# First q and k loads with long runs, one transfer a tile, and the heads turned by a product each

## The chip, the cores and the metric

The kernel runs on one core of one Trainium2 chip. The metric is device microseconds of one launch. Three runs of the kernel before gave 815.03, 815.05 and 818.45 us, median 815.05.

## The reference, cut to what matters

Windowed attention (batch 4, 8 heads, 576 positions, head size 64) feeds two MLPs of 2304 tokens, one after the other. The first four heads of a batch see the last 32 positions, the other four every fourth of the last 128.

```python
scores = scale * np.matmul(q, k.transpose(0, 1, 3, 2))
scores = np.where(masks[None, :, :, :], scores, -1000000000.0)
attn = softmax(scores)                      # written out in the reference
attn_out = np.matmul(attn, v)
x = attn_out.transpose(0, 2, 1, 3).reshape(B * S, H * D)
h = x @ w_in; g = np.maximum(0.01 * h, h); x = g @ w_out
a = x @ w1; b = x @ w2; out = ((a * b) @ w3) @ w_out2
```

q, k and v come as 32-bit floats, the weights as 64-bit floats, which the kernel turns into pairs of 32-bit parts (high and low).

## The kernel before

Two heads make a pair and share the 128 partitions, 64 for each. A batch has four pairs: two of the dilated kind, two plain ones. For the first batch the kernel loads q and k by `load_qk`: eight tiles (q and k of four pairs, m = 0 to 7), each of 288 KB, by two DMAs, one for each head (L345). On n partitions (72 for the dilated pairs, 96 for the plain ones) lie c rows of each head (8 or 6), the two heads side by side in every row, so that each run of the transfer is one head's row of 64 floats, 256 bytes. `turn_rows` then turns such a tile so that the head size lies on the partitions: one TensorE transposition for each c (L397), 128 wide, both heads at once, 8 or 6 a tile, into a pair of PSUM banks; a copy on ScalarE or VectorE (L404) takes it to `qT` or `kT`. Later batches use other functions (`load_halves`, `turn_halves`).

Each pair is worked in two rounds (rows 0 to 319 and 320 to 575), so the first batch has eight rounds n = 0 to 7: scores by products (L420, `ps_s`), mask and scale on VectorE (L435), the maximum (L440), the exponential on ScalarE (L448 in one piece after a subtraction on GpSimd, or L456 in pieces), the sum, its reciprocal, the division on GpSimd (L469), a transposition on TensorE (L485, `ps_p`), a copy (L489), and the products with v (L506, `ps_o`). The result goes into `x` as a high part (L529) and a low part (L532).

Beside this the weights' blocks are loaded (`load_cols` L141 for w_in, `load_rows` L138 for w_out) and converted: a scaling (L113, or L111 on ScalarE), two steps on ScalarE (L165, L167), a shift (L154), an addition (L171), and then the two parts (L116, L118). As soon as four x tiles and the first blocks are there, the products of the first MLP begin (L126 to L128, first into `ps_early`).

The order on every engine is written out by hand: the string `START` has one letter for each step, and each engine takes its steps in that order. `L` takes the next load of the string `LOADS`; `~` is a product of the identity with itself whose result nobody reads (L1503, `warm`); `T` and `Y` are the two halves of `turn_rows`; `S M X q E w` the steps of the scores, `V x y` those of the values, `Q` an early product of the MLP. Loads go out on SyncE's queue (SP), but for the tile that `ON_SCALAR` names, q of the third pair, whose two DMAs ScalarE issues. Strings like `X_ON`, `P_ON` and `MLP_CONV` say which engine makes a step (A ScalarE, D VectorE, G GpSimd).

In what follows T0 to T7 are the eight turns of the first batch, in the order q, k of the first pair, q, k of the second, and so on, and S0 to S7 and V0 to V7 the scores and values of the eight rounds; on TensorE they come as T0 T1 S0 T2 S1 T3 S2 T4 S3 T5 V0 V1 T6 S4 T7 S5 V2 S6 S7 V3 ... V7.

Of the kernel before, what the change touches and what calls it, by code (L numbers as in the profile page):

```python
# [8 lines left out]
F32 = mybir.dt.float32  # L9
# [19 lines left out]
def tile_window_attention_two_mlps(  # L29
# [14 lines left out]
    nc = tc.nc  # L44
    P = 128
    B, H, S, D = q.shape
# [5 lines left out]
    NF = F1 // P  # L52
# [77 lines left out]
    def parts(t, *idx):  # L130
        return tuple(t[(slice(None), i, *idx)] for i in range(2))

    def rows(t, off, dims):
        return bass.AP(t.tensor, t.offset + off, dims)


    def load_rows(raw, src, i):
        nc.sync.dma_start(raw, src[i * P : (i + 1) * P, :])  # L138

    def load_cols(raw, src, i):  # L140
        nc.sync.dma_start(  # L141
            raw.rearrange("p (c f) -> p c f", f=P),
            src[:, i * P : (i + 1) * P].rearrange("(c p) f -> p c f", p=P),
        )
# [29 lines left out]
    def run(steps):  # L174
# [3 lines left out]
    engine_of = {"A": nc.scalar, "D": nc.vector, "G": nc.gpsimd}  # L178
    FOLD_CONV = ("GAD",)
    P_ON = "AADAAAAADAADDDAAAAAAAAAAAAAAAAAA"  # L180
    X_ON = "AADADADDADADDAAAAAAAAAAAAAAAAAAA"
    ONE_EXP = (0, 1, 3, 6, 11, 13, 16, 17, 19, 20, 27, 28, 29, 31)
    GS_ON = {
# [7 lines left out]
    }  # L191
    TURN_ON = "AAAADDAA"
    MLP_CONV = (
        "GDG DAG DDD DAD DAD DAD AAD DDD DAD AAD DAG DAD DAG DAD DAD GAD "
        "AAD AAD AAD DDD GAG AAG GAG DDD AAD ADD GAD DAD DAD AAD AAD GAD "
        "GAD GAD GAD GAD GAD GAD GAD GAD"
    ).split()
    LAST_CONV = ("AAD",)
# [1107 lines left out]
    with ExitStack():  # L1306
# [54 lines left out]
        for f in range(NF + AHEAD):  # L1361
# [14 lines left out]
        runs += [(c, 0, NF) for c in range(2, NCH)]  # L1376
        turns = [(c, f, f0, f1) for c, f0, f1 in runs for f in range(f0, f1)]
        START = (
            "~~~L~L~~~~LTLL~Y~~TY~~~SLTMXSY~LqTMXLE~q~Y~wESRNPwTRML~XNCSYLqEwPMTCLXLVVYqxRxTyEwNy"
            "SYLTRLMLNXLY~LqEPCSPGDwMVALRXCSNLxBL~MqyEwPUSVGLXCLRq~AM~DxVNEy~BXwPqEwGL~R~D~N~Cx~G"  # L1380
            "RADPNyVCIVBUPOx~LCy~IVxUGQQQHOyAxyDIBQQQHAGLOBUAHLUIOgclgIcDJBOgGlLUAHDIFHGAcglBOcHB"
            "LUlgLIDHGLgOAUGHDgIAGHOBDALUBGJDILUBOILJUcLAOlBGGJgclLAIHBDOZgAczUHBlDIGgUJAOIDGBOJc"
            "DAJcBlUGlHIcDlAOgJBDUgLGUJLIcUAlIHOBDLOIUJgGOIJAGBOHALDcclGBDUlAJDIUBOHgIcLGZUzlHAOI"
            "DBGJgUAOgcJIDlcBGOALHBlUGFJgcLABDLlSILUSLOMHXDqEwIMHFgcXHGLlLgDAOqEwJRGUNAJIRDBNcOBP"
            "UJgLGcIAUOBHDIGCAHgOBlcDlGPUgHAlIDUBJOILUGOJCcGAgDlIBDOAHcLUBlIJUgOILO|JcFHlLSSMVMVg"
            "clJXxqEywXFHqxLREyNHgwcRlPgNJCFLPZHczlCHggFVVxLJxLyyJclFJLclSLSMXHMqEwXJqgRcHENwlPgR"
            "HcNClPgJCVclVxyJxGyADBULJHIOgclHGHgDAclBHgULIOJgHZczlSgGSMADHXMBXqEwLUHIOgRqEwNHGRPJ"
            "ANCDBPcULJClIOgJclVVcgGxHAlyxDBGyULHADIOgBHULIOJLJclgGJcADlBJcglLUHcIOlHgHgGJADBJULc"
            "FIOJlLcglHcLlJgHclFSSMMJgLclHXFHgqXLHgqEwHERwNJRNFJcLlJcglJgcFlLHZczlHJgPgFCLHclHgSS"
            "MJFXLJcqEwMlXPFHCqgLRJEcNwlJcRglNVcVxlJyxyPclHCSgSMXHMqXPgEHCwqEwRNHVgRNVxLHyxyPJCLS"  # L1390
            "clSMgFJXLMJqEwcFPlXLJCcRlqEwNJcglRJcNlVFxVxHyLyLPgJCclPFHCLVgcxVlyJxyLHHgclHSgSgMHXM"
            "qEwXRHqEwNPRJCNScSlMFMJgLHZczFPJClXLXqEwVclRgxVLxNyygqEwRNFJPcJClFHgJclSclSMHMXXqPgq"
            "HECwERwNVgxVRyJxLyNPcHlCPgHCSSMVMVHXqEwXqRExNxJywyRNPcJlCPcJClVV^LLLLLLLpgrgclprprJ0"
            "01Jd1dc2Ll23LxHyxy3HJgc4gl0561d2Wc3LlW4prLpH0561L2d45grWW6L0L3d12W3Jp44LrWp0Jr51L6d2"
            "Wclpr0pL5r6dL1L2WeLfH33pr4pWg0L5drLHL6142c3LlgHWpWrpWr540L61d2L03pgrpL5HrW61JL2dJLpc"
            "rLlgWclWp3rWLp4erL5H0f61d2W3LJ4gprLLpHri5c0jl61k2dWg3LmWJp4pLr05r61L2cdWl3LWp4prW0L5"
            "rH61L2d3LWpWpgLHr4r50eL6fd142W0p3561rdWpr24JH3cLWlW56pLrpLgrL4W56pWrprWW!JeLLfLJcLlJ"
            "caglboJchlLnHaHobhgclJnL7g8J9$cla%bHo&h*nLH+-agcblJ=o<hngJLca7l8boH9$h%JnL&gclaH*ob+"
            "hJ-n=gc<Hla7boHhgcl8L9$JnL%a&gbJco*lh+HLnHg-=J<c7al8ob9hH$nLgH%a&gocl*b+Jg-Hh=cnL<li"
            "aH7j8kgH9boh$nLm%aJ&boc*h+JlncL-lJg=g<Hc7al8ob9H$h%gnLJ&a*obJ+-chJl=Lng<cHalc7blHo8h"  # L1400
            "9$nJ%a&bJ*oh+gJn-cg=Hlc<l7H8g9$cH%gl&J*+-Jc=l<@JstgHclvssJgctlHvtvJgsscltJvJ#tsvtivj"
            "km"
        )
        LOADS = (
            "0123a45b67wcwwwwdww8wwwwwwwwwwwwwwwwwew9AwwwwwwwBfCDEFwghwwwwwwwiGHIjJKLMNOPklQRoSTp"
# [53 lines left out]
        with tc.manual_schedule():  # L1459
# [5 lines left out]
            for x in START:  # L1465
                if x == "L":
                    y = next(feed)
                    if y == "w":
                        conv.fetch()
                    elif y == "y":  # L1470
                        conv3.fetch()
                    elif y == "z":
                        load_wo2(next(wo2_no))
                    elif y == "x":
                        conv4.fetch()
                    elif y in "rs":
                        load_y("rs".index(y))
                    elif y in QK:
                        load_qk(QK.index(y))
                    else:  # L1480
                        load_v("abcdefghijklmnop".index(y))
                elif x == "|":
                    raw_es.close()
                    gs_es, gs_p = pool("gs", "left")
                    gs_t.append(gs_p.tile([P, 6 * HM], F32R, name="gs"))
                elif x == "^":
                    att_es.close()
                    fold_es, fold = pool("fold", "right")
# [73 lines left out]
```

## Time and profile before

| | us |
|---|---|
| median of three runs | 815.05 |
| the profiled execution's own time | 814.0 |
| its span | 812.2 |
| TensorE busy | 798.0 (98%) |
| VectorE busy | 535.8 (66%) |
| ScalarE busy | 418.2 (51%) |
| GpSimd busy | 195.9 (24%) |
| first product of the MLP starts | 40.06 |

In the span's 40 slices of 20.3 us TensorE is busy for 8 tenths in the first two and for 9 or more from then on, but for the last (7). The chain that ended last is 82% TensorE. The page's list of queues has nearly all bytes on one of them (173.69 of 175.79 MB), which takes 69.5% of the sixteen DMA engines' time. Busy time on TensorE includes the products that nobody reads.

### The profile page before, as it was taken

How to read it: one execution, taken by the hardware profiler on the slowest of the kernel's cores; microseconds unless marked ns; L12 is line 12 of the kernel's file. 1: busy time of each engine (PE TensorE's matmuls, PEld its weight loads, DVE VectorE, ACT ScalarE, POOL GpSimd, SP SyncE). 2: the span in 40 equal slices, each digit the busy share in tenths (PEclk: the TensorE clock that was granted, in tenths of full speed). 3: DMA queues.
4: the chain of work that ended last, by engine and by line, in shares of the span. 5: the costliest groups of instructions: out<-in, count | busy, mean ns of one | idle time of the engine just before them, and what ended most of it. 6: DMA issues, size and time to landing. Idle time of an engine off the chain costs nothing.

```text
span 812.2 us, 16134 instructions
## 1 busy us (share of the span) xinstructions
PE 798.0 (98%) x5806; PEld 774.1 (95%) x5806; DVE 535.8 (66%) x1063; ACT 418.2 (51%) x954; POOL 195.9 (24%) x223
## 2 busy tenths in 40 slices
PE   8899999999999999999999999999999999999997
PEld 7799999999999999988989999999999999999997
DVE  4899997553555354567784777567869658466446
ACT  4799983452134352556664677554555235333341
POOL 4404421343332334431312210000110300121013
PEclk9999999999999999999999999999999999999999
DMA  6996846346552531477856789539999999889884
GB/s 154 254 322 210 258 116 187 94 143 174 136 155 68 136 102 27 131 175 216 241 174 232 258 277 302 200 112 338 358 382 375 304 305 308 253 253 284 301 253 89
DMA packets 162831, 175.79 MB, mean 216 GB/s; under 512 B 67520, under 2 KB 116160, under 8 KB 162752
## 3 DMA queue, kind: packets, MB, share of 16 engines
q1 hardware_dynamic: 158368, 173.69, 69.5%
q10 hardware_dynamic: 4384, 1.08, 0.6%
q8 instruction: 46, 0.75, 0.4%
q14 instruction: 33, 0.27, 0.1%
HBM read 137.89 MB, written 36.83 MB: 215 GB/s over the span
## 4 chain that ended last, share of the span: by engine, by line
PE 82%; ACT 5%; DVE 4%; SPq 3%; DMA 3%; issue 2%; POOL 0%; ACTq 0%; DVEq 0%; POOLq 0%
PE ps_x L126 7%; PE ps_h L126 7%; PE ps_x L127 7%; PE ps_x L128 7%; PE ps_h L127 7%; PE ps_h L128 7%; PE ps_b L127 3%; PE ps_b L126 3%; PE ps_b L128 3%; PE ps_s L420 2%; PE ps_o L506 2%; PE ps_a L126 2%; PE ps_a L127 2%; PE ps_a L128 2%; PE ps_p L485 2%
## 5 line engine op out<-in xcount | busy, mean ns | idle before, releaser
L126 PE MATMUL ps_h<-x,win 128*128 128x384 f32 (+2 forms) x440 | 139.5, 317 | 0.0
L128 PE MATMUL ps_h<-x,win 128*128 128x384 f32 (+2 forms) x440 | 137.5, 313 | 0.0
L127 PE MATMUL ps_h<-x,win 128*128 128x384 f32 (+2 forms) x440 | 137.5, 312 | 0.0
L126 PE MATMUL ps_x<-gs,wout 128*128 128x384 f32 (+2 forms) x356 | 114.5, 322 | 0.0
L128 PE MATMUL ps_x<-gs,wout 128*128 128x384 f32 (+2 forms) x356 | 112.4, 316 | 0.0
L127 PE MATMUL ps_x<-gs,wout 128*128 128x384 f32 (+2 forms) x356 | 112.4, 316 | 0.0
L118 POOL TENSOR_TENSOR gs<-g,gs 128x384 fp32r<-128x384 f32 (+2 forms) x69 | 65.8, 953 | 146.5 <-DVE gs L116 138.1
L577 ACT ACTIVATE g<-ps_h 128x384 f32<-128x384 f32 (+2 forms) x110 | 48.1, 438 | 100.6 <-PE ps_h L128 72.3
L126 PEld LDWEIGHTS ps_h<-x,win 128*128 128x128 f32 x440 | 83.1, 189 | 1.3
L127 PEld LDWEIGHTS ps_h<-x,win 128*128 128x128 f32 x440 | 83.1, 189 | 0.3
L128 PEld LDWEIGHTS ps_h<-x,win 128*128 128x128 f32 x440 | 83.1, 189 | 0.0
L118 POOL TENSOR_TENSOR p<-t,p 128x384 fp32r<-128x384 f32 x12 | 12.6, 1046 | 256.8 <-DMA place<-ws_dram 96.5
L126 PEld LDWEIGHTS ps_x<-gs,wout 128*128 128x128 f32 x356 | 67.1, 189 | 1.2
L127 PEld LDWEIGHTS ps_x<-gs,wout 128*128 128x128 f32 x356 | 67.2, 189 | 0.3
L128 PEld LDWEIGHTS ps_x<-gs,wout 128*128 128x128 f32 x356 | 67.1, 189 | 0.0
L116 DVE CAST gs<-g 128x384 fp32r<-128x384 f32 (+2 forms) x70 | 24.6, 352 | 57.7 <-PE ps_x L128 43.0
L456 ACT ACTIVATE s<-s,nmax 128x96 f32<-128x96 f32 x83 | 30.0, 364 | 21.8 <-DVE nmax L440 21.7
L127 PE MATMUL ps_b<-ys,place 128*128 128x384 f32 x120 | 40.2, 335 | 0.7 <-DVE ys L118 0.7
L126 PE MATMUL ps_b<-ys,place 128*128 128x384 f32 x120 | 40.1, 334 | 0.0
L128 PE MATMUL ps_b<-ys,place 128*128 128x384 f32 x120 | 40.1, 334 | 0.0
L435 DVE SCALAR_TENSOR_TENSOR s<-ps_s,masks 128x384 f32<-128x384 f32 (+2 forms) x40 | 19.8, 512 | 28.3 <-PE ps_s L420 27.9
L469 POOL TENSOR_TENSOR s<-s,rec 128x480 f32<-128x480 f32 (+1 forms) x32 | 30.0, 939 | 31.1 <-DVE rec L467 27.1
(253 smaller groups left out, 2115.9 us busy)
## 6 DMA issues: line engine op xcount, KB each, us to landing
place<-ws_dram SPq DMA_DIRECT2D x140, 256.0 KB
place<-wps_dram SPq DMA_DIRECT2D x84, 256.0 KB
ws_dram<-ws SPq DMA_DIRECT2D x24, 512.0 KB
raw<-in_moe_w_in_dram SPq DMA_DIRECT2D x16, 512.0 KB
raw<-in_moe_w_out_dram SPq DMA_DIRECT2D x16, 512.0 KB
rawf<-in_moe_w_dram SPq DMA_DIRECT2D x64, 128.0 KB
wo2f<-wo_dram SPq DMA_DIRECT2D x32, 256.0 KB
rawl<-in_moe_w_dram SPq DMA_DIRECT2D x16, 512.0 KB
```

The lines of the kernel that those rows point to most:

```text
L116: copy_on(e_hi)(hi, src)
L118: e_lo.tensor_tensor(lo, src, hi.bitcast(F32), op=ALU.subtract)
L126: nc.tensor.matmul(ps, a[1], b[0], start=first, stop=False, skip_group_check=seeded)
L127: nc.tensor.matmul(ps, a[0], b[1], start=False, stop=False, skip_group_check=seeded)
L128: nc.tensor.matmul(ps, a[0], b[0], start=False, stop=last, skip_group_check=seeded)
L420: nc.tensor.matmul(ps[j * QB : (j + 1) * QB, i - bl.start], qt[d, i * QB : (i + 1) * QB], kt[d, first_key(i, plain) : first_key(i, plain) ...
L435: nc.vector.scalar_tensor_tensor(s[:, a:z], ps[:, a:z], SCALE, mk, op0=ALU.mult, op1=ALU.add)
L456: nc.scalar.activation(s[:, i], s[:, i], AF.Exp, bias=nmax[:, i : i + 1], accum_out=total[:, i : i + 1])
L469: nc.gpsimd.tensor_tensor(s, s, rec[:, :nb].unsqueeze(2).to_broadcast([P, nb, KB]), op=ALU.mult)
L485: nc.tensor.transpose(pss[g][:, i - i0], s[:, i], ident)
L506: nc.tensor.matmul(ps[j * D : (j + 1) * D, i * QB : (i + 1) * QB], vt[i][:, h + j, :], t[:, i, j * QB : (j + 1) * QB], start=True, stop=True,)
L577: nc.scalar.activation(g, ps, AF.Prelu, alpha=SLOPE)
```

## The change

`load_qk` keeps the two heads apart in the tile (`[P, 2, 8, D]` in place of `[P, 8, 2, D]`) and brings both by one DMA, whose runs are a partition's c rows of one head in one piece: 2 KB for the dilated pairs, 1.5 KB for the plain ones. Since a head's row no longer lies beside the other's, `turn_rows` has a product with the identity for each head and row, 64 wide, into its own 64 partitions: 16 or 12 products in place of 8 or 6 transpositions. ScalarE issues three of the eight tiles now (q of the first pair, q and k of the last); the others go out on SP. Four of the 31 products that nobody reads are left out, some letters of `START` stand elsewhere, two casts of x (rounds 4 and 7) go from VectorE to ScalarE (`X_ON`), and four blocks of weights share their conversion among the engines in another way (`MLP_CONV`).

```diff
+    ON_SCALAR = ("k3", "q0", "q3",)
...
     def load_rows(raw, src, i):
-        nc.sync.dma_start(raw, src[i * P : (i + 1) * P, :])
+        block_queue[0].dma_start(raw, src[i * P : (i + 1) * P, :])
...
-    X_ON = "AADADADDADADDAAAAAAAAAAAAAAAAAAA"
+    X_ON = "AADAAADAADADDAAAAAAAAAAAAAAAAAAA"
...
-        "GDG DAG DDD DAD DAD DAD AAD DDD DAD AAD DAG DAD DAG DAD DAD GAD "
-        "AAD AAD AAD DDD GAG AAG GAG DDD AAD ADD GAD DAD DAD AAD AAD GAD "
+        "GDG DAG DDD DAD DAD DDG AAD DDD DAD AAD DAG DAD DAD DAD DAD DAD "
+        "AAD ADD AAD DDD GAG AAG GAG DDD AAD ADD GAD DAD DAD AAD AAD GAD "
...
-    ON_SCALAR = ("q2",)
...
-        t = win_p.tile([P, 8, 2, D], F32, tag="win", name=f"{nm}{pi}", bufs=NF)
-        for j in range(2):
-            queue_of(nm + str(m // 2)).dma_start(
-                t[:n, :c, j, :], rows(src, o + j * S * D, [[c * D, n], [D, c], [1, D]])
-            )
+        t = win_p.tile([P, 2, 8, D], F32, tag="win", name=f"{nm}{pi}", bufs=NF)
+        queue_of(nm + str(m // 2)).dma_start(
+            t[:n].rearrange("p j c d -> p j (c d)")[:, :, : c * D],
+            rows(src, o, [[c * D, n], [S * D, 2], [1, c * D]]),
+        )
...
-                src = t[:n, g * (c // 2) + c1].rearrange("p j d -> p (j d)")
-                nc.tensor.transpose(ps[:, g, c1 * n : (c1 + 1) * n], src, ident[:n, :n])
+                for j in range(2):
+                    nc.tensor.matmul(
+                        ps[j * D : (j + 1) * D, g, c1 * n : (c1 + 1) * n],
+                        t[:n, j, g * (c // 2) + c1], ident[:n, :n], start=True, stop=True,
+                    )
...
         START = (
-            "~~~L~L~~~~LTLL~Y~~TY~~~SLTMXSY~LqTMXLE~q~Y~wESRNPwTRML~XNCSYLqEwPMTCLXLVVYqxRxTyEwNy"
+            "~~~L~L~~~~LTLL~Y~TY~SLTMXSMYLqTX~LEq~Y~wESRNPwTRMSL~XNYCLqEwPMTCLXLVVYqxRxTyEwNyLSYL"
...
                     if y == "w":
+                        block_queue[0] = queue_of(f"w{conv.fetched}")
                         conv.fetch()
+                        block_queue[0] = nc.sync
```

`queue_of("w0")` and so on name no tile of `ON_SCALAR`, so the weights' blocks stay on SP.

TensorE at its start, before: the turns are L397 (`ps_qT`, `ps_kT`), the scores L420 (`ps_s`).

```order
L1503 MATMUL warm<-ident 128x128 x8
L397 MATMUL ps_qT_182<-ident,q_168 128x72 x8
L1503 MATMUL warm<-ident 128x128 x3
L397 MATMUL ps_kT_208<-ident,k_172 128x72 x8
L1503 MATMUL warm<-ident 128x128 x3
L420 MATMUL ps_s_222<-kT_217,qT_204 64x96 x10
L397 MATMUL ps_qT_236<-ident,q_179 128x72 x8
L420 MATMUL ps_s_249<-kT_217,qT_204 64x96 x8
L1503 MATMUL warm<-ident 128x128
L397 MATMUL ps_kT_265<-ident,k_191 128x72 x8
```

The same place now (the lines are 2 to 6 higher):

```order
L1509 MATMUL warm<-ident 128x128 x8
L399 MATMUL ps_qT_179<-ident,q_168 64x72 x16
L1509 MATMUL warm<-ident 128x128 x2
L399 MATMUL ps_kT_211<-ident,k_171 64x72 x16
L1509 MATMUL warm<-ident 128x128
L425 MATMUL ps_s_231<-kT_228,qT_208 64x96 x10
L399 MATMUL ps_qT_244<-ident,q_177 64x72 x16
L425 MATMUL ps_s_265<-kT_228,qT_208 64x96 x8
L399 MATMUL ps_kT_281<-ident,k_196 64x72 x16
```

A turn has 16 instructions where it had 8 and four products that nobody reads are gone.

ScalarE at its start, before: the copies L404 of the first turns and, between the second and the third, the two loads L345.

```order
L404 ACT_TABLE_LOAD
L404 COPY qT_204<-ps_qT_182 128x576
L404 COPY kT_217<-ps_kT_208 128x576
L345 DMA q_233<-in_q_dram 96x6x64 x2
L404 COPY qT_258<-ps_qT_236 128x576
L448 ACTIVATE s_245<-s_245 128x480
```

ScalarE at its start now:

```order
L346 DMA q_168<-in_q_dram 72x2x512
L409 ACT_TABLE_LOAD
L409 COPY qT_208<-ps_qT_179 128x576
L409 COPY kT_228<-ps_kT_211 128x576
L409 COPY qT_276<-ps_qT_244 128x576
L453 ACTIVATE s_261<-s_261 128x480
L409 COPY kT_310<-ps_kT_281 128x576
L453 ACTIVATE s_274<-s_274 128x384
L346 DMA q_367<-in_q_dram 96x2x384
```

The load between the copies is gone; one stands ahead of everything else, and two later ones behind the exponentials of the first two rounds.

SP from its start to the first block of weights (L141), before:

```order
L345 DMA q_168<-in_q_dram 72x8x64 x2
L345 DMA k_172<-in_k_dram 72x8x64 x2
L345 DMA q_179<-in_q_dram 72x8x64 x2
L345 DMA k_191<-in_k_dram 72x8x64 x2
L381 DMA v_0_194<-in_v_dram 96x4x64 x2
...
L345 DMA k_261<-in_k_dram 96x6x64 x2
...
L345 DMA q_330<-in_q_dram 96x6x64 x2
L345 DMA k_351<-in_k_dram 96x6x64 x2
L141 DMA raw_378<-in_moe_w_in_dram 128x4x128
```

SP now, to the same block (L149):

```order
L346 DMA k_171<-in_k_dram 72x2x512
L346 DMA q_177<-in_q_dram 72x2x512
L346 DMA k_196<-in_k_dram 72x2x512
L383 DMA v_0_198<-in_v_dram 96x4x64 x2
...
L346 DMA q_242<-in_q_dram 96x2x384
L346 DMA k_278<-in_k_dram 96x2x384
...
L149 DMA raw_410<-in_moe_w_in_dram 128x4x128
```

Fourteen issues of q and k stood ahead of the first block of weights; five do now. The v loads between them are the same twelve.

## Rows read from the trace of the kernel before

**Rows 1.** The page's busy time of each engine.

```profile
PE 798.0 (98%) x5806; PEld 774.1 (95%) x5806; DVE 535.8 (66%) x1063; ACT 418.2 (51%) x954; POOL 195.9 (24%) x223
```

**Rows 2.** Windows: stretch, length, busy PE, PEld, DVE, ACT, POOL; clock, DMA share, GB/s.

```profile
30.00:40.00 10.00, 8.87 (x129) 7.14 (x123) 9.37 (x27) 8.16 (x27) 5.28 (x5) 1.00 1.08 260
40.06:812.19 772.13, 764.68 (x5368) 745.82 (x5364) 508.84 (x992) 393.69 (x878) 177.39 (x185) 1.00 0.70 217
```

**Rows 3.** Timeline of TensorE: start, us, line, op, shape [idle before, releaser].

```profile
5.48 0.69 PE L397 MATMUL ps_qT<-ident,q 72*128 72x72 f32 x8 [0.61 <-DMA q<-in_q_dram]
6.01 0.88 PE L1503 MATMUL warm<-ident 128*128 128x128 f32 x6
...
8.69 1.04 PE L420 MATMUL ps_s<-kT,qT 64*64 64x96 f32 x20
9.67 0.72 PE L397 MATMUL ps_qT<-ident,q 72*128 72x72 f32 x8
...
12.32 0.73 PE L397 MATMUL ps_kT<-ident,k 72*128 72x72 f32 x8 [0.70 <-ACT qT L404]
...
13.77 1.04 PE L420 MATMUL ps_s<-kT,qT 64*64 64x96 f32 x20
...
15.89 0.66 PE L397 MATMUL ps_qT<-ident,q 96*128 96x96 f32 x6
16.38 0.41 PE L1503 MATMUL warm<-ident 128*128 128x128 f32 x2
...
18.60 1.27 PE L506 MATMUL ps_o<-pT,v 96*64 96x64 f32 x36
20.57 0.69 PE L397 MATMUL ps_qT<-ident,q 96*128 96x96 f32 x6 [0.70 <-DVE x L532]
...
23.66 1.04 PE L420 MATMUL ps_s<-kT,qT 64*64 64x96 f32 x20
...
25.20 0.80 PE L506 MATMUL ps_o<-pT,v 96*64 96x64 f32 x20
27.32 0.88 PE L420 MATMUL ps_s<-kT,qT 64*64 64x96 f32 x16 [1.32 <-DVE total L464]
...
31.64 0.80 PE L506 MATMUL ps_o<-pT,v 96*64 96x64 f32 x20
32.38 0.49 PE L1503 MATMUL warm<-ident 128*128 128x128 f32 x2
...
37.58 0.78 PE L506 MATMUL ps_o<-pT,v 96*64 96x64 f32 x8 [0.39 <-DMA v<-in_v_dram]
...
40.06 0.41 PE L126 MATMUL ps_early<-x,win 128*128 128x320 f32 x1
```

**Rows 4.** Timeline of SP's queue: start, us, line, load, count.

```profile
0.74 1.92 SPq L345 DMA_DIRECT2D q<-in_q_dram  x2
...
16.68 1.24 SPq L345 DMA_DIRECT2D q<-in_q_dram  x2
17.97 1.30 SPq L345 DMA_DIRECT2D k<-in_k_dram  x2
19.32 0.62 SPq L141 DMA_DIRECT2D raw<-in_moe_w_in_dram  x1
```

**Rows 5.** Timeline of ScalarE, with the loads that it issues (ACTq).

```profile
6.21 0.64 ACT L404 COPY qT<-ps_qT 128x576 f32<-128x576 f32 x1 [4.19 <-PE ps_qT L397]
...
9.57 2.02 ACTq L345 DMA_DIRECT2D q<-in_q_dram  x2
11.63 0.64 ACT L404 COPY qT<-ps_qT 128x576 f32<-128x576 f32 x1 [2.99 <-PE ps_s L420]
```

**Rows 6.** Timeline of GpSimd near 26 us.

```profile
25.42 0.67 POOL L113 TENSOR_SCALAR pair<-raw 128x512 f32<-128x512 f32 x1 [2.31 <-DMA raw<-in_moe_w_in_dram]
```

**Rows 7.** Timeline of VectorE, at 26 and at 34 us.

```profile
26.12 0.43 DVE L154 TENSOR_SCALAR pair<-pair 128x512 int32<-128x512 int32 x1 [1.64 <-POOL pair L113]
...
34.26 0.48 DVE L529 CAST x<-ps_o 128x320 fp32r<-128x320 f32 x1
```

More of the change, by code (lines that the diff above doesn't have):

```diff
@@ L131, in parts, with queue_of @@
         return tuple(t[(slice(None), i, *idx)] for i in range(2))
+    ON_SCALAR = ("k3", "q0", "q3",)
+    def queue_of(name):
+        return nc.scalar if name in ON_SCALAR else nc.sync
+    block_queue = [nc.sync]
     def rows(t, off, dims):
@@ L137, in load_rows @@
     def load_rows(raw, src, i):
-        nc.sync.dma_start(raw, src[i * P : (i + 1) * P, :])
+        block_queue[0].dma_start(raw, src[i * P : (i + 1) * P, :])
     def load_cols(raw, src, i):
-        nc.sync.dma_start(
+        block_queue[0].dma_start(
             raw.rearrange("p (c f) -> p c f", f=P),
@@ L270, in tile_window_attention_two_mlps @@
     nat_t, v_t, qk_t = {}, {}, {}
-    ON_SCALAR = ("q2",)
-    def queue_of(name):
-        return nc.scalar if name in ON_SCALAR else nc.sync
     order, seq = [], []
@@ L1378, in tile_window_attention_two_mlps @@
         START = (
-            "~~~L~L~~~~LTLL~Y~~TY~~~SLTMXSY~LqTMXLE~q~Y~wESRNPwTRML~XNCSYLqEwPMTCLXLVVYqxRxTyEwNy"
[L1380 to L1402, printed above, removed]
+            "~~~L~L~~~~LTLL~Y~TY~SLTMXSMYLqTX~LEq~Y~wESRNPwTRMSL~XNYCLqEwPMTCLXLVVYqxRxTyEwNyLSYL"
+            "TRLMLNXYLqEPCSPGwLDMVARXCNSLxBL~~MqyEwPUSVGLXCLRq~AM~DxVNE~BXwPqEwGGL~Ry~D~N~Cx~RADP"
@@ new lines, in tile_window_attention_two_mlps @@
+            "NyVCIVBUPOx~LCy~VxUGQQQIHOyAxyIDBQQQHALOBUGUAHLIOgclgIcDJBOgGAlLUHDIFHGAcglBOcHBLUlg"
+            "LIDHGLgOAUGHDgIAGHOBDALUBGJDILUBOILJUcLAOlBLGJgclGIAHDBOZgAczHlUIDGBgJUAODIGBJOcADJc"
+            "BlUGlHIcDlAOgJBDUgLGUJLIcUAlIHOBDLOIgUGOIAGBOHALJJDcclGBDUlAJDIBOHgcULIGZUzlHAOIDBGJ"
+            "JgUAOgcIDlcBGOAHLBlUGFgcLABDLJlSILUSLOMHXDqEwIMHFgcXHGLlLgDAOqEwJRGUNAJIRDBNcOBPUJgL"
+            "GcIAUOBHDIGCAHgOBlcDlGPUgHAlIDUBJOILUGOJCcGAgDlIBDOAHcLUBlIJUgOILO|JcFHlLSSMVMVgclJX"
@@ new lines, in tile_window_attention_two_mlps @@
+            "xqEywXFHqxLREyNHgwcRlPgNJCFLPZHczlCHggFVVxLJxLyyJclFJLclSLSMXHMqEwXJqgRcHENwlPgRHcNC"
+            "lPgJCVclVxyJxGyADBULJHIOgclHGHgDAclBHgULIOJgHZczlSgGSMADHXMBXqEwLUHIOgRqEwNHGRPJANCD"
+            "BPcULJClIOgJclVVcgGxHAlyxDBGyULHADIOgBHULIOJLJclgGJcADlBJcglLUHcIOlHgHgGJADBJULcFIOJ"
+            "lLcglHcLlJgHclFSSMMJgLclHXFHgqXLHgqEwHERwNJRNFJcLlJcglJgcFlLHZczlHJgPgFCLHclHgSSMJFX"
+            "LJcqEwMlXPFHCqgLRJEcNwlJcRglNVcVxlJyxyPclHCSgSMXHMqXPgEHCwqEwRNHVgRNVxLHyxyPJCLSclSM"
@@ new lines, in tile_window_attention_two_mlps @@
+            "gFJXLMJqEwcFPlXLJCcRlqEwNJcglRJcNlVFxVxHyLyLPgJCclPFHCLVgcxVlyJxyLHHgclHSgSgMHXMqEwX"
+            "RHqEwNPRJCNScSlMFMJgLHZczFPJClXLXqEwVclRgxVLxNyygqEwRNFJPcJClFHgJclSclSMHMXXqPgqHECw"
+            "ERwNVgxVRyJxLyNPcHlCPgHCSSMVMVHXqEwXqRExNxJywyRNPcJlCPcJClVV^LLLLLLLpgrgclprprJ001Jd"
+            "1dc2Ll23LxHyxy3HJgc4gl0561d2Wc3LlW4prLpH0561L2d45grWW6L0L3d12W3Jp44LrWp0Jr51L6d2Wclp"
+            "r0pL5r6dL1L2WeLfH33pr4pWg0L5drLHL6142c3LlgHWpWrpWr540L61d2L03pgrpL5HrW61JL2dJLpcrLlg"
@@ new lines, in tile_window_attention_two_mlps @@
+            "WclWp3rWLp4erL5H0f61d2W3LJ4gprLLpHri5c0jl61k2dWg3LmWJp4pLr05r61L2cdWl3LWp4prW0L5rH61"
+            "L2d3LWpWpgLHr4r50eL6fd142W0p3561rdWpr24JH3cLWlW56pLrpLgrL4W56pWrprWW!JeLLfLJcLlJcagl"
+            "boJchlLnHaHobhgclJnL7g8J9$cla%bHo&h*nLH+-agcblJ=o<hngJLca7l8boH9$h%JnL&gclaH*ob+hJ-n"
+            "=gc<Hla7boHhgcl8L9$JnL%a&gbJco*lh+HLnHg-=J<c7al8ob9hH$nLgH%a&gocl*b+Jg-Hh=cnL<liaH7j"
+            "8kgH9boh$nLm%aJ&boc*h+JlncL-lJg=g<Hc7al8ob9H$h%gnLJ&a*obJ+-chJl=Lng<cHalc7blHo8h9$nJ"
@@ L1403, in tile_window_attention_two_mlps @@
+            "%a&bJ*oh+gJn-cg=Hlc<l7H8g9$cH%gl&J*+-Jc=l<@JstgHclvssJgctlHvtvJgsscltJvJ#tsvtivjkm"
         )
```

## The prediction

> **What bounds the kernel now.** I read the page's busy times first: TensorE works for 798.0 of 812.2 us, and no other engine for more than two thirds [rows 1]. The windows then say where the rest is: from 40.06 us, where the first product of the MLP starts, to the end TensorE is busy for 764.68 of 772.13 us, at a granted clock of 1.00 [rows 2]. None of the edits takes work from that stretch (the letters that move there and the four conversion patterns shift work among engines that TensorE doesn't wait for). So the change can move the end only by moving the start of the MLP, and its worth is read from the first 40 us alone.
>
> In these 40 us the timeline of TensorE is a row of short pieces with idle time between them, and three kinds of stop show: for q or k to land (0.61 us at 5.48), for ScalarE (0.70 at 12.32), and 1.32 us at 27.32 [rows 3]. The queues say why. SP issues one load after the other from 0.74 us on, and the first block of weights is the 27th, at 19.32 [rows 4]; ScalarE stands in its own two loads from 9.57 to 11.59 while a turned tile waits for its copy, which starts at 11.63 [rows 5]; and the block issued at 19.32 reaches GpSimd at 25.42 after 2.31 us of idling [rows 6], so VectorE gets its word at 26.12 after 1.64 us [rows 7], and the scores at 27.32 come late by it. The change goes at all three. What it pays with is TensorE's time.
>
> **Price of a turn.** Eight transpositions take 0.53 us from their start to the next instruction (5.48 to 6.01), six of the 96-wide ones 0.49 (15.89 to 16.38) [rows 3]. The new products do not occur in the trace. The nearest are the values: a product from 96 partitions into one 64-wide half, the halves in turn, as the new ones; ten of 64 columns take 0.74 us (31.64 to 32.38), 74 ns each. The scores have 64 partitions and 96 columns: ten in 0.98 us (8.69 to 9.67), 98 ns [rows 3]. Between the two, 72 columns are about 80 ns and 96 are 98, so a turn is 16 x 80 = 1.28 us or 12 x 98 = 1.18, dearer by 0.75 or 0.69: 4 x 0.75 + 4 x 0.69 = 5.76 us more on TensorE. Against it stand four dropped products that nobody reads, at most 0.29 us each (three in 0.88 [rows 3]), which filled waiting time in any case. Ends for the price: from below a turn costs what it costs now (the halves run wholly beside each other); from above, a product has the price of a full-width one, (0.88 - 0.16) / 3 = 0.24 us for 128 columns, where 0.16 is what a group's last instruction adds (0.69 - 0.53). By width that is 0.135 or 0.18 us, 2.16 us a turn. I take 1.28 and 1.18, since the values' rows have the same halves.
>
> The Trainium skill, "FP8 and Floating Point Precision", section "TensorE Precision Notes", has a rule that speaks against the change: true 32-bit products take four passes through the array. As an estimate by that page a turn of 16 products would be 16 x 4 x 72 columns at 2.4 GHz = 1.92 us; the sum below would come out some 5 us later, as in the costly rival. The trace does not agree for products in halves: at four passes one of 64 columns would be 107 ns, and the row has 74.
>
> **The chain, stage by stage.** *To the first scores.* T0 could start at 4.87 (5.48 less 0.61 of waiting) if q landed by then. Both tiles' loads now go out side by side, from ScalarE and from SP, with one issue each where q alone took two, 1.92 us [rows 4], so I take that it does; at worst it starts at 5.48 as now. Then T0 1.28 + 0.16, copy 0.64 with 0.04 ahead of it (5.48 + 0.69 = 6.17, copy at 6.21 [rows 5]) to 6.99; T1, which waits for that copy, 7.03 to 8.47; copy to 9.15; S0 at 9.2. Now it is 8.69: **0.5 later**. The longer turns stand one behind the other here and eat what the loads give.
>
> *To S2.* T2 starts 0.98 after S0, at 10.2, and ends at 11.6; ScalarE is free, so its copy starts at 11.66, where it starts at 11.63 today. T3 at 12.34 (today 12.32), done at 13.8, copied at 14.46, S2 at 14.5 (today 13.77): **0.7 later**. The removed stop on ScalarE has paid for T2 and no more.
>
> *To S5.* Two 96-wide turns lie ahead of the first values: + 1.38, less up to 1.0 of idle and of a dropped filler there, so V0 comes 1.1 to 2.1 after today's 18.60. T6 stops today for 0.70 us; the view names VectorE, but its tile's loads were issued until 17.92, and 17.92 + 2.8 (5.48 - 2.66, the same lag as at the first tile) = 20.7, which is its start [rows 3, 4]. That stop goes. T6 and T7 add 1.38, one filler goes (0.25). S5: 23.66 + 1.5 to 2.6.
>
> *To S6.* Here the raw block is paid back. Of the 14 issues of q and k ahead of it five remain. Going by the rows at 16.68 and 17.97, a tile's two took 1.24 to 1.92 us [rows 4], so nine fewer save 5.6 us at least, and the block lands before 20, not at 25.42. GpSimd, VectorE and so TensorE do not stop for it. S6 then follows S5 by its own work, S5 to the end of V2, 2.3 us (23.66 to 26.00), and the mask step behind S5: at 27.4 to 28.4, against 27.32. I take **0.5 later**.
>
> *To the MLP.* From there VectorE is what fills up: 9.37 of 10 us from 30 to 40 [rows 2]. One cast of 0.48 us leaves it (34.26 [rows 7]) and another of the same kind; ScalarE has 8.16 of 10 and takes them. The stop of 0.39 us for the last v tile (37.58) should go, as its loads are issued earlier. Together 0.4 to 0.9 gained, 0.6 taken.
>
> **Sum.** + 0.5 - 0.6 = - 0.1 us: the MLP starts at 40.0. The profiled execution took 814.0 us, its span and 1.8 around it, so 813.9 by it. The median shown, 815.05, lies 1.05 above that execution; the same shift makes it **815.0**. By the bounds of each stage alone it is - 0.8 to + 0.7.
>
> **Rivals.**
>
> *Cheap turns.* If a turn costs what it costs now, all three stops are pure gain: S0 at 7.7 (- 1.0), no wait for a load at T6, none for the raw block. S6 then comes at 25.3 to 25.6 (VectorE's 1.64 and some start), with 0.6 behind it: 2.3 to 2.6 us, **812.6**. For it: nothing forbids that the halves overlap. Against it: the values' rows show 74 ns in this form already. It stays within what can be told from no change.
>
> *Costly turns (slower).* TensorE works in order, and T4 to T7 stand ahead of values and scores that ScalarE and VectorE wait for. My chain has used up nearly all idle time by S5, so from there each further tenth on a turn is passed on: 8 x (price - 1.23). At 2.16 us that is 7.4, **822.3**; at the end where it just decides, 4 us more, a turn takes about 1.75. For it: it is the price of full-width products, and an array that changes between widths may lose time at each change. Against it: rows at 31.64 and 32.38, where half-width goes over to full width with no gap.
>
> *The loads do not come earlier.* The DMA engines are full from 30 to 40 (share 1.08 [rows 2]); if they and not the issues hold back the raw block, GpSimd waits as now. But S5 is late already, and the raw block at 25.4 would then just meet it: S6 at 27.8, v's 0.39 stays: + 0.5, **815.5**.
>
> *All stops close up.* To be faster by over 4 us the MLP would have to start before 36.0. VectorE alone has 9.37 us of work in the last ten, so cheap turns would have to meet a freed VectorE as well: **810.5**, little speaks for it.
>
> **How the numbers follow.** Forecast 0.60, cheap turns 0.18, costly turns 0.10 (of it 0.07 beyond 4 us), loads not earlier 0.08, all stops 0.04. About 0.5%, 4 us, is what a measurement of this kernel can tell from no change, so faster 0.04, slower 0.07, same 0.89. The range goes from the cheap turns' 812.4 up into the costly ones as far as a turn of about 1.6 us, + 3: 818.0. The likeliest case's own range is 814.2 to 815.8.
>
> **What would show it.** Right: turns of 1.2 to 1.4 us on TensorE; the third turn's copy at about 11.7; no stop of GpSimd for the raw block; the S6 scores between 27.3 and 28.4; the first early product within 1 us of 40.06, and from there to the end the same 772 us. Wrong: turns of 0.6 us (cheap) or from 1.7 (costly); a raw block that lands after 24; or a stretch behind the MLP's start that is longer or shorter than 772 us by more than 1, which my argument rules out.

## Result and profile after

The changed kernel takes 824.15 us (median of 14 runs, 816.01 to 825.61); the kernel before, on the same chip, 814.88 (14 runs). The ratio taken over all runs is 1.0096, 95% interval 1.0077 to 1.0115 (that of the two medians is 1.0114): slower by 0.96%, where no change was forecast, and outside the range, which ended at 818.0. The profiled execution took 824.9 us, its span is 823.1.

The runs lie in two groups: three at 816.0 to 817.7 and eleven at 822.4 to 825.6. With the repetitions told below, 20 of 27 executions of this code lie above 821 us. Only four of the 27 were profiled, the one shown here and three below. The three of the upper group ran most or all of their first four turns at the lower of TensorE's two clock levels, the one of the lower group ran none so. That the clock of the first 24 us is what tells the groups apart is read from these four; for the other 23 it is inferred from their times.

Busy time of each engine after, as in [rows 1]:

```profile
PE 810.1 (98%) x5966; PEld 783.9 (95%) x5966; DVE 535.1 (65%) x1064; ACT 417.6 (51%) x954; POOL 195.6 (24%) x222
```

TensorE is busy for 12.1 us more; the other engines do what they did.

Windows after, columns as in [rows 2]: a stretch of the start, then from the first product of the MLP to the end.

```profile
12.00:20.00 8.00, 7.99 (x103) 7.03 (x102) 3.40 (x7) 1.47 (x4) 1.81 (x2) 1.00 0.92 204
...
46.87:823.10 776.23, 766.14 (x5368) 745.58 (x5364) 508.92 (x996) 393.34 (x877) 177.18 (x184) 1.00 0.69 213
```

The MLP starts at 46.87, 6.81 us later than in [rows 2], and the stretch behind it takes 776.23 us, 4.10 more. Together that is the 10.9 us between the two profiled executions. From 12 to 20 us TensorE is busy for 7.99 of 8.00 us, where it had idle time before.

The timeline of TensorE after shows on what. Columns as in [rows 3].

```profile
1.36 3.79 PE L1509 MATMUL warm<-ident 128*128 128x128 f32 x16 [1.36 <-POOL ident masks.py:199]
6.04 2.19 PE L399 MATMUL ps_qT<-ident,q 72*64 72x72 f32 x32 [0.89 <-DMA q<-in_q_dram]
...
9.31 2.19 PE L399 MATMUL ps_kT<-ident,k 72*64 72x72 f32 x32
...
12.23 1.86 PE L425 MATMUL ps_s<-kT,qT 64*64 64x96 f32 x20
14.03 2.19 PE L399 MATMUL ps_qT<-ident,q 72*64 72x72 f32 x32
...
17.62 2.19 PE L399 MATMUL ps_kT<-ident,k 72*64 72x72 f32 x32
...
21.32 1.87 PE L425 MATMUL ps_s<-kT,qT 64*64 64x96 f32 x20
23.12 1.06 PE L490 MATMUL ps_p<-ident,s 128*96 128x128 f32 x5
24.11 1.21 PE L399 MATMUL ps_qT<-ident,q 96*64 96x96 f32 x24
...
35.38 0.88 PE L425 MATMUL ps_s<-kT,qT 64*64 64x96 f32 x16
...
46.87 0.41 PE L126 MATMUL ps_early<-x,win 128*128 128x320 f32 x1
```

(A product leaves two records, a transposition one: x32 are 16 products.) The scores are the same instructions in both kernels: 1.04 us in [rows 3], 1.86 here at 12.23. Everything up to 23 us runs at not much over half the rate, the lower of TensorE's two clock levels (1.2 GHz); from 24 us on durations are those of [rows 3] again (2.4 GHz). The column for the granted clock, the last but two in a window, says 1.00 from 12 to 20 us all the same, so at the start of a run the level has to be read from durations of known instructions. T0 to T3 take 2.19 us each in place of 0.7, T4 to T7 1.2 (both with the tail of their last instruction). The lag is 3.5 us at S0, 7.6 at S2, 8.2 at T4, and from there it does not grow: S6 comes 8.1 late, the MLP 6.8.

SP's queue, then ScalarE with the loads that it issues, after (columns as in [rows 4, 5]):

```profile
12.35 0.48 SPq L149 DMA_DIRECT2D raw<-in_moe_w_in_dram  x1
```

```profile
16.26 0.64 ACT L409 COPY qT<-ps_qT 128x576 f32<-128x576 f32 x1 [4.08 <-PE ps_qT L399]
...
19.90 0.33 ACTq L346 DMA_DIRECT2D q<-in_q_dram  x1
```

GpSimd on the first raw block:

```profile
32.37 0.66 POOL L113 TENSOR_SCALAR pair<-raw 128x512 f32<-128x512 f32 x1
```

What the change was to do for the queues it does. The raw block goes out at 12.35, not at 19.32 [rows 4]; GpSimd no longer waits for it [rows 6]; ScalarE's issue takes 0.33 us, not 2.02, and T2's copy waits for TensorE (4.08 us), no more for the issue [rows 5].

### The profile page after: what moved, and what is told of

Same layout as the page of the kernel before. It is cut to its first block, busy times and chain, and to the rows that moved or that the text cites. A ratio compares the mean times of both kernels' runs of the same rounds, so it can differ in the third digit from the quotient of the medians.

```text
span 823.1 us, 16443 instructions
## 1 busy us (share of the span) xinstructions
PE 810.1 (98%) x5966; PEld 783.9 (95%) x5966; DVE 535.1 (65%) x1064; ACT 417.6 (51%) x954; POOL 195.6 (24%) x222
## 4 chain that ended last, share of the span: by engine, by line
PE 81%; DMA 8%; DVE 4%; ACT 3%; issue 2%; SPq 1%; POOL 0%; ACTq 0%; POOLq 0%; DVEq 0%
PE ps_x L126 8%; PE ps_x L127 8%; PE ps_x L128 8%; PE ps_h L126 7%; PE ps_h L127 7%; PE ps_h L128 7%; PE ps_s L425 3%; PE ps_b L127 2%; PE ps_b L126 2%; PE ps_b L128 2%; DMA wo2f<-wo_dram 2%; PE ps_o L511 2%; PE ps_p L490 2%; PE ps_a L126 2%; PE ps_a L127 2%
```

## Experiments

Ratios are against the kernel before on the same chip, with the 95% interval. "Late" is a profiled run in which TensorE runs at least two of its first four turns at the lower level; of a run without a profile the text gives the time.

**The same code, two clocks.** The changed kernel again, unedited, a single run:

> The changed kernel once more, unaltered, for a second profile. Theory of the clock: it shows one of two forms: a rise after 15 us, turns of 2.2 us and 822 to 826, or a rise by 7 us, turns of 1.2 us, an MLP start at 40 to 42 and 815 to 818.

815.98 us. TensorE's timeline:

```profile
5.73 1.22 PE L399 MATMUL ps_qT<-ident,q 72*64 72x72 f32 x32 [0.58 <-DMA q<-in_q_dram]
6.88 0.71 PE L1509 MATMUL warm<-ident 128*128 128x128 f32 x4
...
9.64 1.04 PE L425 MATMUL ps_s<-kT,qT 64*64 64x96 f32 x20 [0.32 <-ACT kT L409]
...
21.82 1.19 PE L399 MATMUL ps_qT<-ident,q 96*64 96x96 f32 x24
22.95 1.04 PE L425 MATMUL ps_s<-kT,qT 64*64 64x96 f32 x20
...
28.31 0.88 PE L425 MATMUL ps_s<-kT,qT 64*64 64x96 f32 x16
...
39.82 0.41 PE L126 MATMUL ps_early<-x,win 128*128 128x320 f32 x1
```

With identical instructions the turns take 1.22 us here and 2.19 there, and the MLP starts 7.05 us earlier. That separates the price of the lower level from all edits: 7.05 us at the MLP's start, of which 0.31 is q, which landed later there. The two executions lie 8.9 us apart (824.9 less 815.98), but the rest, in the stretch behind (776.23 and 774.37), is not shown to be the clock's: the late profile told next takes 773.35 there. By the rows, T0 to T3 take 0.97 longer each, the first three rounds' scores 2.3 together, the unread products and the first transposition of a score 1.8: 8.0 us of dearer work up to 24 us, most of it passed on.

**What the lower level costs in each kernel.** Both kernels without the eight unread products ahead of T0:

```diff
-            "~~~L~L~~~~LTLL~Y...
+            "LLLTLL~Y...
```

In the changed kernel:

> The changed kernel without the eight unread products ahead of the first turn, so that nothing runs on TensorE before the turns. Theory: the first turns run at the lower level in every run, at 2.2 us each, the MLP starts at 43 to 47 us and the median is 820 to 825 us. Rival (the products cost the same 1.2 us wherever they stand, and the 824 us had another cause): turns of 1.2 us, MLP at 39.5 to 41, median 815.5 to 817.

Median 822.66 us (five runs, 821.68 to 826.61), 1.0116 [1.0098, 1.0134]: every run lies over 821. The one profiled is late:

```profile
5.95 2.19 PE L399 MATMUL ps_qT<-ident,q 72*64 72x72 f32 x32 [5.95 <-DMA q<-in_q_dram]
...
23.76 1.21 PE L399 MATMUL ps_qT<-ident,q 96*64 96x96 f32 x24
...
46.54 0.41 PE L126 MATMUL ps_early<-x,win 128*128 128x320 f32 x1
```

In the kernel before:

> The kernel before without the eight unread products ahead of the first turn. Theory: its transpositions cost 1.2 us instead of 0.7 at the lower level, which the idle time of the first 25 us takes up; the MLP starts within 1.5 us of 40.06 and the median is 813 to 816 us. Rival (a late clock costs some 7 us in any kernel): MLP at 45 to 47, median 819 to 823.

Median 815.47 us (12 runs, 813.91 to 816.54), 1.0018 [1.0010, 1.0027].

```profile
5.45 1.19 PE L397 MATMUL ps_qT<-ident,q 72*128 72x72 f32 x8 [5.45 <-DMA q<-in_q_dram]
...
10.28 1.21 PE L420 MATMUL ps_s<-kT,qT 64*64 64x96 f32 x20
11.42 0.72 PE L397 MATMUL ps_qT<-ident,q 72*128 72x72 f32 x8
...
39.25 0.41 PE L126 MATMUL ps_early<-x,win 128*128 128x320 f32 x1
```

By the MLP's start the edit costs the kernel before nothing, and the changed kernel begins it 6.7 us later than in its early run above. Two things differ in the traces. A turn by transpositions is 1.19 us at the lower level, one by products 2.19. And the rise comes within S0, between 10 and 11 us, in the kernel before, but near 23 in the changed kernel, though TensorE has hardly any idle time from 6 us on. So in these two kernels the late clock is dear with the new turns and costs little without them. Why the rise comes so much later is not shown; the two kernels also differ in their loads and their order.

**What makes it late.** Four unread products are gone from the start. They went back in, in two sessions:

```diff
-            "~~~L~L~~~~LTLL~Y~TY~SLTMXSMYLqTX...
+            "~~~L~L~~~~LTLL~Y~~TY~~~SLTMXSMYL~qTX...
```

> The changed kernel with the four dropped products that nobody reads put back where they stood (three after the first turn, three after the second, one before the fourth). Theory of the clock: the wide products between the turns are what raises it when the first eight do not (the products-only kernel, which has them, rose at 6.25 us in its profile); so most runs fall to 815 to 819, the clock rises by 10 us and the MLP starts at 40 to 43. Rival (the late arrival of the first q tile at 6.04 us, and the 0.89 us of idling ahead of it, keeps the clock low, fillers or not): most runs stay at 822 to 826, with the clock rising after 15 us.

Median 816.90 (10 runs; the ratio leaves out one of 826.89), 1.0043 [1.0026, 1.0061]. That seemed to be the answer. But in its profile T0, ahead of which the two codes are the same, already takes 1.22 us. So it ran once more, beside the changed kernel on one chip:

> The changed kernel with the four dropped unread products back, beside e12. Theory: the products behind the first turn make up for a rise that was missed, so the median is 816 to 818 us and at most 2 runs in 10 lie over 820. Rival (the products do not matter, the first rise is chance): the same spread as e12, whatever that is.

> The changed kernel once more, unchanged, timed beside e13 on one chip. Theory: its clock rises late in most executions (turns at 2.2 us), so the median is 821 to 825 us with more than half of the runs over 820. Rival: the two forms seen so far (824 in one session, 815.98 in another) belong to the session, not to the kernel; then the median here is near 816 and e12 and e13 agree within 1 us.

With the products back: 821.08 us, 1.0104 [1.0056, 1.0152], three of six runs at 825.8 to 827.7. The changed kernel: 822.97, 1.0095 [1.0062, 1.0127], four of six over 822. Times of the upper group come with the four products there too, though the run profiled is one of the early ones (815.67): the theory that their loss alone is the cause fell (whether it makes such times more frequent, 20 of 27 against 4 of 16 over 821, mixes sessions and stays open). The profile of the changed kernel taken there shows the place:

```profile
6.17 1.22 PE L399 MATMUL ps_qT<-ident,q 72*64 72x72 f32 x32 [1.05 <-DMA q<-in_q_dram]
...
8.13 1.99 PE L399 MATMUL ps_kT<-ident,k 72*64 72x72 f32 x32
...
45.30 0.41 PE L126 MATMUL ps_early<-x,win 128*128 128x320 f32 x1
```

TensorE was at the higher level at T0 (1.22), for which it had stood still 1.05 us waiting for q, and fell back in T1. So the start was made longer there, with six more unread products ahead of T0, in two sessions, the second beside the changed kernel:

```diff
-            "~~~L~L~~~~LTLL~Y...
+            "~~~L~L~~~~L~~~~~~TLL~Y...
```

> The changed kernel with six more products that nobody reads (128 wide) ahead of the first turn, 14 in place of 8. Theory of the clock: in the profile of the changed kernel TensorE runs at its lower level until about 24 us, since the first eight wide products end before the clock rises and the 64-wide products of the turns do not raise it. Then the longer warm-up lets it rise before the first turn in nearly every run: turns of 1.1 to 1.3 us, MLP start at 40 to 43 us, time 815 to 819, no run near 824. Rival (a turn is as dear as it looks at any clock, 2.2 us): MLP start at 47 to 48, time 824 to 826.

> The changed kernel with six more unread products ahead of the first turn, so that TensorE does not stand still for q there, beside the changed kernel on one chip. Theory (the stop ahead of the first turn is where the early rise is missed or lost): no run over 821.5 us, median 816.5 to 818.5. Rival (the early rise is chance, whatever stands there): as many runs over 822 us as in the changed kernel.

> The changed kernel again, beside the one with six more unread products. By both theories at least a third of its runs lie over 822 us and the median between 818 and 825; if all lie under 820 the two cannot be told apart here.

Six more products: 818.19 us, 1.0050 [1.0033, 1.0067], and 817.91, 1.0047 [1.0031, 1.0064]; the highest of 17 runs is 820.96. The changed kernel beside the second: 824.24, 1.0095 [1.0057, 1.0132], five of six over 821.7, and its profile is late like the first (T0 to T3 at 2.19, the MLP at 46.94). TensorE with six more products, first session:

```profile
1.35 5.29 PE L1509 MATMUL warm<-ident 128*128 128x128 f32 x28 [1.35 <-POOL ident masks.py:199]
6.57 1.22 PE L399 MATMUL ps_qT<-ident,q 72*64 72x72 f32 x32
...
40.58 0.42 PE L126 MATMUL ps_early<-x,win 128*128 128x320 f32 x1
```

No run lies over 821 (three of the 17, not profiled, lie between 820.4 and 821), and both profiles have T0 at 1.22. The six products fill the stop for q and also make the unread work longer; which of the two decides was not told apart. With the clock up 0.5% stays: in the first session's profile the MLP starts 0.5 us later than in [rows 3], and the stretch behind takes 774.30, 2.2 more than in [rows 2]. But the six products have a price of their own: T0 starts at 6.57, at 5.73 in the early run of the changed kernel. The changed kernel's own seven executions under 821 lie 1.1 to 5.1 us above the median of the kernel before beside them, the middle one 1.9 (0.2%); its other twenty lie 7.6 to 12.1 above. So the upper group makes most of the loss.

**One part of the change at a time.** The products alone (heads apart, two DMAs a tile as before, order and queues of before), and the same with the long loads, all on SP:

```diff
+        t = win_p.tile([P, 2, 8, D], F32, tag="win", name=f"{nm}{pi}", bufs=NF)
...
+                for j in range(2):
+                    nc.tensor.matmul(...)
```

> The kernel before with the heads apart and a product each in the turns, and nothing else: two DMAs a tile on the queues of before, the order, the 31 unread products and the conversions of before. Theory of the clock: the wide products ahead of the first turn are the same eight, so in most runs the clock stays low through the turns: turns of 2.2 us, MLP start at 46 to 48, time 821 to 825, with some runs at 815 to 818. Rival (the loads or the new order cost the time, not the turns): 814 to 817 in all runs, turns of 1.2 us.

816.12 us, 1.0033 [1.0016, 1.0050], one run of 12 over 821, where I expected most. T0 starts at 5.07 with no stop ahead of it, and the clock rises in it (1.77 us): so the expectation that the narrow products do not raise it fell as well.

> The products-only kernel with one DMA of long runs a tile, all on SP: order, fillers and patterns of before, ScalarE issues no load. Theory of the clock: first q lands by 5 us, the clock rises at 4 to 8 us, turns of 1.2 us, MLP start at 39 to 41, time 813 to 817, like the products alone (816.1). Rival (long runs on the DMA engines make the products' kernel slow): 820 or more.

816.71, 1.0035 [1.0014, 1.0056]. The profile is of its slowest run, 822.31:

```profile
5.07 2.19 PE L397 MATMUL ps_qT<-ident,q 72*64 72x72 f32 x32
...
14.26 1.22 PE L397 MATMUL ps_qT<-ident,q 72*64 72x72 f32 x32
...
43.57 0.42 PE L126 MATMUL ps_early<-x,win 128*128 128x320 f32 x1
```

This run is late with no stop ahead of T0, with all 31 unread products and with the order of before, so neither the stop nor the four lost products is needed for a late clock.

The changed kernel with the order of before (`START`, `X_ON`, `MLP_CONV`):

> The changed kernel with the order string, the two casts and the conversion patterns of before; the loads, their queues and the turns stay changed. Theory of the clock: with the 31 fillers the clock rises by 10 us in most runs, time 815 to 819. Rival (late q tile): most runs at 821 to 825 with a clock that rises after 15 us.

816.70, 1.0052 [1.0031, 1.0073], none of six runs over 820.5; MLP at 40.29. T0 has its stop for q here too (0.86 us) and runs at 1.22: the stop alone does not make a run late. Over 821 us lie 20 of 27 executions of the changed kernel, four of 16 with the four products back, none of 17 with six more, none of six here, and one of 12 and one of ten in the two versions before. What decides how often the clock is late stays open; the changed kernel with nothing but its first q back on SP was not run.

The kernel before with the change's order, casts and conversion patterns:

> The kernel before with the order string, the engines of two casts and the conversion patterns of the changed kernel; loads and turns as before. Theory of the clock: order and patterns are worth little, time 813 to 817, MLP start at 39 to 41. Rival (the new order or fewer unread products cost the time, and give the two long waits at 435 and 572 us of the changed kernel's trace): 818 or more, with these waits.

816.78, 1.0028 [1.0009, 1.0047]. Its profile, of the slowest run (821.33), is late, with transpositions of 1.2 us to 17.6 us, and the MLP still starts at 40.10: once more a late clock without a price at that point. This run loses its time behind it: the stretch takes 779.45 us. TensorE waits 1.9 us for a block of w3 and 2.5 for `ps_c`, the two waits that the rival named (0.5 and 1.8 us in the profile after), and behind each the granted clock falls (0.72 on average from 412 to 418 and from 568 to 574 us). So a long run can also have this cause.

The kernel before with the four products dropped, nothing else:

```diff
-            ...LTLL~Y~~TY~~~SLTMXSY~LqTMXLE...
+            ...LTLL~Y~TY~SLTMXSYLqTMXLE...
```

> The kernel before with four of the products that nobody reads left out (two after the second turn, one after the first, one before the fourth), and nothing else. Theory of the clock: with fewer wide products between the turns the clock rises late in more of the runs, but short turns at the lower rate cost little (the order-only kernel rose at 17.6 us and still began the MLP at 40.1): median 814 to 816.5, the top of the runs up to 820. Rival (only the narrow turns need the fillers): 813 to 814, as the kernel before, clock up by 5 us.

815.12, 1.0013 [1.0003, 1.0024]. Here TensorE fell back to the lower level behind a stop of 1.60 us and stayed there to 16.2 (three unread products, six records, in 1.58 us, not 0.88):

```profile
12.54 1.00 PE L397 MATMUL ps_kT<-ident,k 72*128 72x72 f32 x8 [1.60 <-ACT qT L404]
13.34 1.58 PE L1503 MATMUL warm<-ident 128*128 128x128 f32 x6
```

The MLP starts at 38.70 all the same. All 12 runs lie between 813.3 and 816.5.

**The loads without the products.** The changed kernel with the heads side by side, one DMA a tile in runs of 256 bytes and the old transpositions:

```diff
-            rows(src, o, [[c * D, n], [S * D, 2], [1, c * D]]),
+            t[:n, :c], rows(src, o, [[c * D, n], [D, c], [S * D, 2], [1, D]])
...
+                nc.tensor.transpose(ps[:, g, c1 * n : (c1 + 1) * n], src, ident[:n, :n])
```

> The changed kernel with the turns of before: both heads side by side again, one 128-wide transposition for a row, still one DMA a tile (its runs are 256 bytes again) and the queues and the order of the change. Theory of the clock: it rises at 4 to 6 us as in the kernel before; turns of 0.5 us, MLP start at 37 to 40, time 811 to 815. Rival (the queues and the order make it slow): 819 to 824 with 0.5 us turns.

817.36, 1.0046 [1.0026, 1.0065]; the profile is of its slowest run. The lower level lasts to 13.5 us, T7 stops 1.92 us for a k that ScalarE issues at 18.30, behind that stop the clock falls back (scores of 1.86 us at 27.36), and the MLP starts at 42.42. The expected gain did not come.

The same single DMA in the kernel before, all on SP, with turns and order untouched:

```diff
-    ON_SCALAR = ("q2",)
+    ON_SCALAR = ()
...
-        for j in range(2):
...
+            t[:n, :c], rows(src, o, [[c * D, n], [D, c], [S * D, 2], [1, D]])
```

> The kernel before with one DMA a tile in place of two (both heads side by side, runs of 256 bytes), all on SP: order, fillers, turns and patterns of before. Both theories hold that fewer issues and a ScalarE that issues nothing cost nothing here: MLP start at 38.5 to 40, time 811 to 814, same as before or 1 to 2 us faster. If it is slower by over 1 us, merging the loads hurts by itself (the first q tile lands later, since the next ones share the DMA engines with it).

812.66 us (12 runs), 0.9990 [0.9982, 0.9999]: the one version below the kernel before, by 0.1% and hardly beyond its interval. Its timeline of TensorE:

```profile
20.23 0.69 PE L396 MATMUL ps_qT<-ident,q 96*128 96x96 f32 x6 [0.56 <-DMA q<-in_q_dram]
...
37.43 0.42 PE L126 MATMUL ps_early<-x,win 128*128 128x320 f32 x1
```

The MLP starts 2.63 us earlier than in [rows 3]; the stretch behind it is 0.7 longer (772.87 us), with a new wait for a block of w_in:

```profile
PE ps_h L126 <- DVE win L118: 0.9, 1, 0.9
```

(The columns are those of the waits below.)

**The conversions.** That version with `X_ON` and `MLP_CONV` of the change:

> The kernel before with one DMA a tile on SP (which began the MLP 2.6 us earlier and gave 1.6 us of it back to a wait of TensorE for a block of w_in) and with the two casts and the conversion patterns of the change. If VectorE's work is what gives the gain back, moving the casts to ScalarE keeps up to 1 us more: 811 to 812.5. If the patterns were made for another order, it is 812.5 to 814.

814.83, 1.0013 [1.0001, 1.0026], an expectation missed: against 0.9990, from another session, the casts and patterns cost about 0.2%. The profile, of its second fastest run, does not show where: the MLP starts 0.5 us later (37.97) and the stretch behind is the same (772.83). TensorE's waits behind the start of the MLP (waits for: total us, times, longest), before, after and in this version:

```profile
PE ps_b L126 <- DVE ps_c L997: 0.2, 1, 0.2
```

```profile
PE ps_b L126 <- DVE ps_c L1002: 1.8, 1, 1.8
PE ps_b L127 <- DVE ys L118: 0.7, 1, 0.7
PE ps_wp L126 <- DVE w3T L118: 0.6, 1, 0.6
PE ps_wp L126 <- ACT wo L116: 0.5, 1, 0.5
PE ps_x L126 <- DVE x L116: 0.4, 1, 0.4
```

```profile
PE ps_b L126 <- DVE ps_c L996: 1.0, 1, 1.0
PE ps_h L126 <- DVE win L118: 0.3, 1, 0.3
```

Twelve profiled kernels have the change's patterns, and the wait for `ps_c`, late in the second MLP, is 0.9 to 2.5 us in all of them. Seven have those of before, and it is 0.6 or less. So a wait at some 570 us goes with the patterns (or the two casts, which were always changed with them). Six of those seven (not the profile of before itself) instead stop 0.9 us for a block of w_in early in the MLP, this version 0.3, so the patterns also buy something. By what way they delay `ps_c` was not tried.

## Why the prediction was wrong

**The profile's bound and the queues: right.** TensorE still bounds the kernel and the stops for SP's and ScalarE's issues went as said. One step fails here: T0 was to start at 4.87, since q and k go out side by side from ScalarE and SP with one issue each. It stops 0.89 us for q and starts at 6.04. In all nine profiles in which ScalarE issues the first q and T0 waits for it, T0 starts at 5.73 to 6.17; in the eight in which SP issues it first, at 4.95 to 5.49. The same long loads all on SP had T0 at 5.07 with no stop, so the delay comes with giving the first q to ScalarE's queue while k goes out beside it on SP, and neither the long runs nor the single DMA makes it alone. By what way was not tried.

**The price of a turn: right at the level it was read at, wrong in the run.** With the clock up a turn is 1.22 us with its last instruction's tail, 1.15 without (1.28 was taken) and 1.13 at 96 columns (1.18 taken); neither the cheap nor the costly end holds, nor the 1.92 us of the four passes. The step that failed stands ahead of it, and the prediction takes it without saying so: that TensorE is at the higher level from T0 on, so that durations of rows behind 5.48 us hold for the changed start. The clock of 1.00 that it quotes is read behind 40.06 us. [Rows 3] begin behind the rise; the sixteen records of unread products ahead of them took 3.51 us there and 3.79 after, mostly at half rate in both. In two of the four profiled executions all of the first four turns took 2.19 us, in a third T1 to T3 took 1.99 to 2.19; 20 of 27 executions lie with these three by their time. The term of the sum that fails by it is 1.28 for a turn: it was 2.12 (14.03 to 16.15).

**The chain by stages: right with the clock up.** Forecast against the run with the early rise: S0 9.2 and 9.64, T2 10.2 and 10.62, S6 between 27.3 and 28.4 and 28.31, the MLP at 40.0 and 39.82. There is some luck in it: T0 started 0.86 late, and turns that were 0.13 and 0.05 us cheaper than taken made up for a part. In the late profile S0 is at 12.23, S6 at 35.38, the MLP at 46.87.

**The costly rival gave 822.3 us from turns of 2.16.** Both numbers came near, for a reason it did not have: its price was one of the instruction (full width, or changes between widths), for all eight turns. The runs show 1.2 us for the same instructions at the higher level, and 2.19 for the first four turns only. That it came near is luck. Its other part, that idle time is used up and each further tenth is passed on, is what happens: 8.0 us of dearer instructions, and 0.31 of q's later landing, move the MLP by 7.05.

**The stretch behind the MLP's start: wrong.** 772 us was said to be the same to within 1, because the conversions shift work among engines that TensorE doesn't wait for. It is 776.23 in the late profile and 774.37 with the clock up. The wait for `ps_c` is 1.6 or 1.1 us more than before, and goes with the patterns in all profiles. The rest (0.5 for `wo`, TensorE busy 1.5 longer) varies between profiles of the same code and stays open. The patterns are not the only way to a longer stretch: the long loads all on SP, with the patterns of before, took 776.96 in their profile, the kernel before without its first eight products 774.47.

**The chance: wrong.** 0.07 was given to slower, since no rival had the clock in it. The Trainium skill has it: "TensorE: Matmul & The Clock Gate", section "Part 1: The HAM clock gate", says that the throttled clock is the default, that activity releases it, and that the number of products at the lower clock differs between runs of one kernel; the cost of the ramp it puts below 1% of a typical span. The trace agrees on the first and the third: the run starts at the lower level, and the same code has its first turns at 2.19 and at 1.22 us. On the second it shows less than the sentence says: TensorE was busy for 7.99 of 8.00 us from 12 to 20 us and stayed at the lower level until near 24. The size is near the bound: 7.05 us of 823.1, 0.9%, by the MLP's start.

## What to carry to other kernels

Before pricing an added instruction by rows, look at which clock level those rows ran, and price the start at both levels; the same table row can be worth 1.2 or 2.2 us. A start that depends on an early clock rise is settled in many runs and in several sessions: ten runs of one session here pointed to a cause that a second session took away. A change that removes idle time from an engine also removes the cover under which a late clock cost little. And whether a first tile lands earlier on another queue deserves a run of its own: here it landed later.

## What the runs showed that was not expected

- TensorE stayed at the lower level while busy for 7.99 of 8.00 us (12 to 20 us after), and rose between 10 and 11 us in the kernel before without its first eight products.
- It fell back behind short stops: in T1 after 1.05 us of standing still ahead of T0, behind 1.60 us at 12.54 and 1.92 at 25.89, and, far into a run, behind 1.9 and 2.5 us near 412 and 570 us. Stops of 0.58 to 0.89 us ahead of T0 were followed by early and by late runs.
- The granted clock of the windows shows 1.00 over stretches in which known instructions take 1.8 times as long (scores 1.86 and 1.04 us). In the run that rose first and then fell in T1 the same column shows 0.50 from 9 to 10 us.
- A 32-bit product into one half costs 72 ns at 72 columns (1.15 / 16) and 94 at 96 (1.13 / 12): close to its width, so two half-width products cost about twice one full-width transposition (0.53 us for eight).
- One DMA of a q or k tile takes its queue 0.31 to 0.62 us to issue in the profile after, where two took 1.24 to 2.02 [rows 4, 5]. It is not the number alone: two DMAs a tile with the heads apart took 0.78 to 1.59, one DMA with the heads side by side 0.59 to 1.63, and one of the long ones, all on SP, 1.55.
